# Sliding-window attention and a low-rank mixer: K and Q loaded in long rows, transposed on VectorE as bf16 pairs, scores on 32-row array tiles

## The chip, the cores and the metric

One core of a Trainium2 chip. The metric is the device time of one execution in microseconds (us), lower is better. Times come with a state (slow means over 1.5% above the fastest run of the same kernel); all timed runs used here are of the fast state, except that a run with a single execution has no state. "Span" is the profiled execution from its first to its last instruction, about 1.6 to 2.1 us shorter than its time. The "granted clock" is the share of TensorE's full clock that the profile shows as granted: 1 is full, 0.5 half. Engines: PE is TensorE's matmuls, PEld its weight loads, DVE VectorE, ACT ScalarE, POOL GpSimd.

## The reference, cut to what matters

```python
# q, k, v: (8 batches, 8 heads, 576, 64); window 64
scores = scale * q @ k^T;  mask: 0 <= i - j < 64
x = softmax(scores) @ v            # -> (8, 576, 512)
u = x + (U V applied along the sequence)
out = u + relu(u @ w_ch1) @ w_ch2  # 512 -> 2048 -> 512
```

All 4608 tokens go through the last line in nine chunks of 512. Attention of batch c+1 is woven into the matmuls of chunk c, in numbered slots; batch 0's stands alone ahead of chunk 0. I call that part the start-up; it ends with the first up-projection matmul (tile `psA`).

## The kernel before

K and Q are loaded in bf16 with the sequence on partitions, in pieces of 64 elements (groups of six rows for batches 0 and 1), transposed on TensorE against an identity, and evacuated by ScalarE (K) and VectorE (Q). A score matmul takes 128 keys, two heads on two 64-row tiles of the array. Cuts are marked `...`.

```python
def tr(src, j, wide=False):        # batches 2 to 7 take this path
    ...
    tp = ps_tp.tile([P, NT, P], BF16, name="tpn", tag="tp")
    for t in range(NT):
        nc.tensor.transpose(tp[:, t, :], src[:, t, 2*j : 2*j+2, :]..., ident[:])
def TK(j): nc.scalar.copy(out=like(kt[j][:]), in_=tr(kb, j))
def TQ(j): nc.vector.tensor_copy(out=like(qt[j][:]), in_=tr(qb, j, ...))
def scores(sc, n, j, blk):
    for g in range(2):             # two heads, rows 0-63 and 64-127
        nc.tensor.matmul(sc[:, g, n*W : (n+1)*W], kt[j][rs, w0 : w0+P],
                         qt[j][rs, blk*W : (blk+1)*W], start=True, stop=True)
PLACE = {"S": [2, 2, 6, 6, 10], "PV": [13, 13, 16, 16, 18],
         "T": [16, 17, 18, 19, 20, 21, 22, 23], ...}   # slot in the chunk
```

`turn_over(n)` issues n filler matmuls whose result nobody reads; they keep TensorE busy in the start-up. In the schedules, `T` or `KT` stands for transposing K and Q, `S` for a piece of scores with its exponential on ScalarE and its mask product on VectorE, `VC` for copies of V, `PV` for a value tile, `U` and `V` for the low-rank mixer, and `UT` for transposing the tokens.

The softmax here doesn't subtract the row's maximum and nothing guards it: scores larger than these inputs give would overflow.

Of the kernel before, what the change touches and what calls it, by code (L numbers as in the profile page):

```python
# [9 lines left out]
ALU = mybir.AluOpType  # L10
# [6 lines left out]
def kernel(  # L17
# [19 lines left out]
    HP = H // 2  # L37
# [3 lines left out]
    GR = 6  # L41
    NGR = 2
    GP = S // GR
# [14 lines left out]
    kg_pool = ctx.enter_context(tc.tile_pool(name="kg", bufs=4))  # L58
# [15 lines left out]

    ident = const.tile([P, P], BF16, name="ident")
    maskA = const.tile([P, 2, NB - 1, W], BF16, name="maskA")
    w1b = const.tile([P, NDC, F], BF16, name="w1b")
    w2b = const.tile([P, NFC, DM], BF16, name="w2b")
    NT = 5
# [7 lines left out]
    vB = [const.tile([P, NFULL, H, VW], BF16, name=f"vB{i}") for i in range(2)]  # L87
    kn = [const.tile([P, NT, H, D], BF16, name=f"kn{i}") for i in range(2)]
    qn = [const.tile([P, NT, H, D], BF16, name=f"qn{i}") for i in range(2)]
    kt = [const.tile([P, S], BF16, name=f"kt{j}") for j in range(HP)]  # L90
    qt = [const.tile([P, S], BF16, name=f"qt{j}") for j in range(HP)]
    pts = const.tile([P, HP, 2, NB, W], BF16, name="pts")

    loaded = {}


    def load_kq(b, split):
        grouped = b < NGR
        if grouped:
            kb = kg_pool.tile([GP, H, GR, D], BF16, name="kg")  # L100
            qb = kg_pool.tile([GP, H, GR, D], BF16, name="qg")
        else:
            kb, qb = kn[b % 2], qn[b % 2]
        loaded[b] = (kb, qb)
        if grouped:
            step = 2 if split else H
            for h0 in range(0, H, step):
                hs = slice(h0, h0 + step)
                for t, src in ((kb, k), (qb, q)):
                    nc.gpsimd.dma_start(  # L110
                        out=t[:, hs, :, :].rearrange("p h c d -> p h (c d)"),
                        in_=src[b, hs, :, :].rearrange("h (p c) d -> p h (c d)", c=GR),
                    )
                    yield
        else:
            for t in range(NT):
                rows = P if t < NFULL else W
                for dst, src in ((kb, k), (qb, q)):
                    nc.gpsimd.dma_start(  # L119
                        out=dst[0:rows, t, :, :],  # L120
                        in_=src[b, :, t * P : t * P + rows, :].rearrange("h p d -> p h d"),
                    )
                yield

    def load_v(b, both=False):
        va, vb = vA[b % 2], vB[b % 2]
        for t in range(NFULL):
            nc.gpsimd.dma_start(  # L128
                out=va[:, t, :, 0:D],
                in_=v[b, :, t * P : (t + 1) * P, :].rearrange("h p d -> p h d"),  # L130
            )
            if both and t > 0:
                nc.gpsimd.dma_start(  # L133
                    out=vb[:, t - 1, :, 0:D],
                    in_=v[b, :, t * P - W : t * P + W, :].rearrange("h p d -> p h d"),
                )
        lo = 0 if both else W
        nc.gpsimd.dma_start(
            out=vb[lo:P, NFULL - 1, :, 0:D],
            in_=v[b, :, NFULL * P - W + lo : S, :].rearrange("h p d -> p h d"),  # L140
        )

    def shift_v(b, copy):
        va, vb = vA[b % 2], vB[b % 2]
        for t in range(NFULL):
            if t > 0:
                copy(out=vb[W:P, t - 1, :, 0:D], in_=va[0:W, t, :, 0:D])
            copy(out=vb[0:W, t, :, 0:D], in_=va[W:P, t, :, 0:D])


    kq0 = load_kq(0, True)
    nc.vector.memset(idle[:], 0.0)  # L152
    nc.vector.memset(ident[:], 0.0)
    next(kq0)
    next(kq0)
# [450 lines left out]
```

## Time and profile before

| | before |
|---|---|
| time, median of 4 runs | 351.89 us (351.63, 351.83, 351.95; one of 492.81 is no fast run) |
| start-up (first `psA`) | 28.5 us |
| chunks 0 to 8 | 40.4, 41.0, 36.6, 36.5, 37.0, 36.5, 34.2, 27.6, 31.6 us |
| DMA packets | 132 thousand |

The chunk times are differences between the first `psA` pieces of the chunks in the chain of waits (a piece there can begin up to 0.2 us after its first matmul); the last goes to the end of the span. Lines of the profile's page, with busy us and share of the span, the granted TensorE clock in 40 slices (9 is 90% or more), and the shares of the chain of waits that ended last:

```profile
span 349.8 us, 7003 instructions
...
PE 332.9 (95%) x2963; PEld 167.0 (48%) x3014; DVE 174.5 (50%) x320; ACT 125.0 (36%) x191; POOL 119.5 (34%) x150
...
PEclk9999999999999999999999999999999999999999
...
PE psU L457 34%; PE psA L435 31%; DMA qg<-in_q_dram 6%; PE tpn L254 5%; PE xr L324 3%; DMA vA_103<-in_v_dram 2%; PE sc L278 2%; PE psv L373 2%; PE tpu L408 2%; PE pshh L353 1%; POOL kg L110 1%; ACT pts L293 1%; POOL qg L110 1%; POOL vA_103 L128 1%; POOL w2b L210 0%
```

TensorE is the limit and has its full clock from start to end. Its timeline, with start, duration, operation, shapes and count (read the distance between starts: a `psA` matmul is drawn 0.38 us long, but the next one starts 0.2155 us after it):

```profile
28.52 4.69 PE L435 MATMUL psA<-uTc,w1b 128*128 128x512 bf16 x21 [0.67 <-ACT uTc L413]
...
185.50 0.41 PE L278 MATMUL sc<-qt_115,kt_111 64*128 64x64 bf16 x16
185.75 0.40 PE L278 MATMUL sc<-qt_116,kt_112 64*128 64x64 bf16 x16
186.08 3.67 PE L435 MATMUL psA<-uTc,w1b 128*128 128x512 bf16 x15
...
208.11 0.44 PE L254 MATMUL tpn<-ident,qn_109 128*128 128x128 bf16 x5
208.39 0.38 PE L457 MATMUL psU<-w2b,c_8_2872 128*128 128x512 bf16 x1
```

The start-up ends at 28.52. 32 score matmuls hold TensorE from 185.50 to 186.08. Five transposes cost 0.28 us, and a batch from 2 on has eight such bursts.

### The profile page before, as it was taken

The page shows a single profiled execution, that of the slowest core. Times are in us where ns is not written, and L with a number is a line of the kernel's source. Part 1 is how long each engine was busy: PE and PEld are TensorE (multiplying, and loading weights), DVE is VectorE, ACT ScalarE, POOL GpSimd, SP SyncE. Part 2 cuts the span into 40 slices and gives each one's busy share as a digit, 9 for nine tenths or more (in the row PEclk, how much of TensorE's full clock was granted, in tenths as well). Part 3 has the DMA queues.
Part 4 walks back from the last instruction along what each step waited for, and adds up shares of the span by engine and source line. Part 5 has one row for each costly group of instructions (what it writes and reads, how often), then busy time and mean ns, then how long its engine had stood idle before and what let it go on. Part 6 is the DMA issues. An engine that isn't in the chain of part 4 may idle for free.

```text
span 349.8 us, 7003 instructions
## 1 busy us (share of the span) xinstructions
PE 332.9 (95%) x2963; PEld 167.0 (48%) x3014; DVE 174.5 (50%) x320; ACT 125.0 (36%) x191; POOL 119.5 (34%) x150
## 2 busy tenths in 40 slices
PE   7978989988999999999999999999999999999995
PEld 3434454444554455545554555445544454444442
DVE  3574257555653755375446545664546554214311
ACT  2632461355332632354225423353335231401300
POOL 8892269989944046605480160000000000000000
PEclk9999999999999999999999999999999999999999
DMA  8999999999999059906995292000010011011011
GB/s 112 166 207 207 198 142 188 167 171 143 149 127 167 2 37 134 187 24 45 108 163 66 15 131 66 32 2 30 32 62 0 32 43 49 0 60 62 0 52 69
DMA packets 132175, 31.89 MB, mean 91 GB/s; under 512 B 121264, under 2 KB 126384, under 8 KB 132144
## 3 DMA queue, kind: packets, MB, share of 16 engines
q0 software_dynamic: 125552, 21.57, 88.7%
q1 hardware_dynamic: 6592, 9.88, 8.2%
q8 instruction: 23, 0.38, 0.4%
q14 instruction: 8, 0.07, 0.1%
HBM read 43.57 MB, written 9.44 MB: 152 GB/s over the span
## 4 chain that ended last, share of the span: by engine, by line
PE 82%; DMA 9%; POOL 4%; issue 2%; ACT 1%; DVE 1%; POOLq 0%; ACTq 0%
PE psU L457 34%; PE psA L435 31%; DMA qg<-in_q_dram 6%; PE tpn L254 5%; PE xr L324 3%; DMA vA_103<-in_v_dram 2%; PE sc L278 2%; PE psv L373 2%; PE tpu L408 2%; PE pshh L353 1%; POOL kg L110 1%; ACT pts L293 1%; POOL qg L110 1%; POOL vA_103 L128 1%; POOL w2b L210 0%
## 5 line engine op out<-in xcount | busy, mean ns | idle before, releaser
L435 PE MATMUL psA<-uTc,w1b 128*128 128x512 bf16 x553 | 129.8, 379 | 2.1 <-ACT uTc L413 0.7
L435 PEld LDWEIGHTS <-w1b 128*128 128x128 bf16 x576 | 54.0, 98 | 62.6 <-issue 2.2
L466 DVE TENSOR_TENSOR osb<-psU,un 128x512 f32<-128x512 f32 x36 | 24.8, 690 | 60.5 <-PE psU L457 54.2
L293 ACT ACTIVATE pts<-sc 128x1024 bf16<-128x1024 f32 x32 | 31.4, 1023 | 17.9 <-PE sc L278 17.9
L294 DVE TENSOR_TENSOR pts<-pts,maskA 128x1024 bf16<-128x1024 bf16 x32 | 22.2, 695 | 17.8 <-ACT pts L293 17.6
L128 POOL DMA_DIRECT2D vA_104<-in_v_dram x16 | 14.2, 889 | 43.7 <-PE xr L324 35.7
L413 ACT COPY uTc<-tpu 128x512 bf16<-128x512 bf16 x27 | 15.8, 585 | 27.9 <-PE tpu L408 27.9
L128 POOL DMA_DIRECT2D vA_103<-in_v_dram x16 | 14.3, 907 | 17.0 <-PE xr L324 16.5
L333 DVE RECIPROCAL rcp<-xr 128x8 f32<-128x8 f32 (+1 forms) x40 | 8.2, 204 | 21.4 <-PE xr L324 21.2
L324 PEld LDWEIGHTS <-pts 128*64 128x64 bf16 x576 | 12.8, 110 | 12.2 <-issue 9.5
L119 POOL DMA_DIRECT2D kn_108<-in_k_dram x15 | 13.0, 866 | 9.0 <-PE tpn L254 8.5
L389 DVE TENSOR_TENSOR un<-psv,xs_102 128x512 bf16<-128x512 f32 (+1 forms) x18 | 11.9, 687 | 7.9 <-PE psv L373 7.9
L408 PEld LDWEIGHTS <-un 128*128 128x128 bf16 x144 | 10.6, 98 | 8.9 <-issue 1.9
L389 DVE TENSOR_TENSOR un<-psv,xs_101 128x512 bf16<-128x512 f32 (+1 forms) x18 | 11.5, 682 | 5.8 <-PE psv L373 5.8
L334 DVE TENSOR_TENSOR xs_102<-xr,rcp 128x512 bf16<-128x512 f32 (+1 forms) x20 | 13.8, 692 | 0.7
L334 DVE TENSOR_TENSOR xs_101<-xr,rcp 128x512 bf16<-128x512 f32 (+1 forms) x20 | 13.8, 690 | 0.7
L500 PE MATMUL unread<-idle 128*128 128x256 bf16 (+1 forms) x46 | 12.5, 371 | 1.6 <-DVE idle L152 1.3
L119 POOL DMA_DIRECT2D kn_107<-in_k_dram x15 | 12.9, 863 | 3.2 <-PE tpn L254 2.5
L119 POOL DMA_DIRECT2D qn_110<-in_q_dram x15 | 13.1, 874 | 1.4 <-PE tpn L254 1.4
L119 POOL DMA_DIRECT2D qn_109<-in_q_dram x15 | 13.0, 867 | 1.2 <-PE tpn L254 0.9
L373 PE MATMUL psv<-hh,vrep 128*128 128x512 bf16 x40 | 12.7, 379 | 0.7 <-DVE un L389 0.6
L133 POOL DMA_DIRECT2D vB_106<-in_v_dram x12 | 10.7, 892 | 6.2 <-DMA w2b<-in_moe_w_ch_dram 4.2
(579 smaller groups left out, 590.8 us busy)
## 6 DMA issues: line engine op xcount, KB each, us to landing
out_dram<-osb SPq DMA_DIRECT2D x36, 256.0 KB, 2.6
vA_103<-in_v_dram POOLq DMA_DIRECT2D x16, 128.0 KB, 6.0
w1b<-in_moe_w_ch_dram POOLq DMA_DIRECT2D x2, 1024.0 KB, 13.7
w2b<-in_moe_w_ch_dram POOLq DMA_DIRECT2D x2, 1024.0 KB, 15.3
vA_104<-in_v_dram POOLq DMA_DIRECT2D x16, 128.0 KB, 5.7
vB_106<-in_v_dram POOLq DMA_DIRECT2D x16, 128.0 KB, 5.9
kn_107<-in_k_dram POOLq DMA_DIRECT2D x12, 128.0 KB, 5.5
qn_109<-in_q_dram POOLq DMA_DIRECT2D x12, 128.0 KB, 5.6
```

What stands on the lines that cost most here:

```text
L119: nc.gpsimd.dma_start(out=dst[0:rows, t, :, :], in_=src[b, :, t * P : t * P + rows, :].rearrange("h p d -> p h d"),)
L128: nc.gpsimd.dma_start(out=va[:, t, :, 0:D], in_=v[b, :, t * P : (t + 1) * P, :].rearrange("h p d -> p h d"),)
L293: nc.scalar.activation(out=dst, in_=sc[:], func=ACT.Exp, scale=scale)
L294: nc.vector.tensor_tensor(out=dst, in0=dst, in1=maskA.rearrange("p g n w -> p g (n w)"), op=ALU.mult)
L324: nc.tensor.matmul(xr[r0 : r0 + W, h // 4, (h % 4) * VW : (h % 4 + 1) * VW], pts[:, h // 2, h % 2, blk, :], rhs, start=True, stop=True,)
L334: nc.vector.tensor_tensor(out=x[lo:hi, t, :, :].rearrange("p (a h) d -> p a h d", a=2), in0=xv[:, :, :, 0:D], in1=rcp[lo:hi].to_broadcast( ...
L373: nc.tensor.matmul(ps[:, n, :], vrep[:, off : off + P], hh["sb"][:], start=True, stop=not on_pe)
L389: nc.vector.tensor_tensor(out=u_tiles[g][rs, :], in0=ps[rs, n, :], in1=xt[n][rs], op=ALU.add)
L408: nc.tensor.transpose(tp[:, dc, :], u_tiles[g][:, dc * P : (dc + 1) * P], ident[:])
L435: nc.tensor.matmul(ps[:], w1b[:, dc, i * P : (i + 1) * P], uTc[:, dc, :], start=(dc == 0), stop=(dc == NDC - 1),)
L457: nc.tensor.matmul(acc[t][:], c1[i][:, t * P : (t + 1) * P], w2b[:, i, :], start=(i == 0), stop=(i == NFC - 1),)
L466: nc.vector.tensor_tensor(out=osb[:], in0=acc[t][:], in1=u_tiles[g][:], op=ALU.add)
```

## The change

The intent is to take the transposes off TensorE. K and Q now arrive as one head per 32-partition quadrant, 18 rows of 64 elements in one stretch per partition. VectorE transposes them as 4-byte words, each a pair of bf16; as the diff's indices have it, the head dimension lands as 32 partitions times 2. A score then needs two accumulating matmuls (`e` = 0, 1) with 32 contracted rows, for 64 keys at a time. The block's shifted copy of V is made by VectorE instead of a second load (for batch 0 instead of GpSimd's copies). The core of the diff, cut:

```diff
-    kb = kg_pool.tile([GP, H, GR, D]); ... per-tile loads of 64-element rows
+    kv = k[b].rearrange("(j i) (p c) d -> (i p) j (c d)", i=NQ, c=RP)
+    nc.gpsimd.dma_start(out=kr[b % 2][:, j], in_=kv[:, j])      # and q
-    TK / TQ: 40 TensorE transposes and 8 evacuations a batch
+    nc.vector.transpose(                                        # KT, 4 a batch
+        out=dst[:, j].rearrange("q (p c) e -> q p (c e)", c=RP).bitcast(U32)
+        .rearrange("q p c -> q c p"),
+        in_=src[odd][:, j, :].bitcast(U32).rearrange("q (c e) -> q c e", e=32))
-    nc.tensor.matmul(sc[:, g, ...], kt[j][rs, w0 : w0 + P], ...)
+    for e in range(2):
+        for half in range(2):
+            for g in range(2):
+                rs = slice((2 * p + g) * 32, (2 * p + g + 1) * 32)
+                nc.tensor.matmul(sc[half*W:(half+1)*W, g, ...],
+                    kt[rs, j, kb*W:(kb+1)*W, e], qt[rs, j, ..., e],
+                    start=(e == 0), stop=(e == 1))
+    pair_v: nc.vector.tensor_copy(vb <- va)                     # VC, 2 or 8 copies
-    "S": [2, 2, 6, 6, 10], ... "T": [16, ... 23]
+    "VC": [0], "S": [1, 3, 5, 7, 9, 11], ... "KT": [13, 15, 17, 18]
 start-up, in short:
+    KT[0:2]; mask set-up; for s in 0, 1: S[s]; turn_over(4)
+    KT[2:4];              for s in 2..5: S[s]; turn_over(4)
+    VC (8 copies); PV; U; V; UT
```

The whole diff holds more that goes with this: VectorE takes 7 instead of 8 of a chunk's 16 relus, batch 1 loses its variant of the stand-alone path, and the first weight is loaded in three pieces instead of two, with the loads in another order.

More of the change, by code (lines that the diff above doesn't have):

```diff
@@ L36 @@
     NB = S // W
-    HP = H // 2
     NDC = DM // P
@@ L40 @@
     VW = D + 1
-    GR = 6
-    NGR = 2
-    GP = S // GR
+    NJ = 2
+    NQ = H // NJ
+    RP = S // 32
+    NPC = 3
+    PB = NJ * NB // NPC
     NFULL = S // P
@@ L57 @@
     const = ctx.enter_context(tc.tile_pool(name="const", bufs=1))
-    kg_pool = ctx.enter_context(tc.tile_pool(name="kg", bufs=4))
     uT_pool = ctx.enter_context(tc.tile_pool(name="uT", bufs=3))
@@ L72 @@
     ctx.enter_context(tc.manual_schedule())
+    U32 = mybir.dt.uint32
+    NT = 5
     ident = const.tile([P, P], BF16, name="ident")
-    maskA = const.tile([P, 2, NB - 1, W], BF16, name="maskA")
+    mask = const.tile([P, NJ * NB, W], BF16, name="mask")
     w1b = const.tile([P, NDC, F], BF16, name="w1b")
     w2b = const.tile([P, NFC, DM], BF16, name="w2b")
-    NT = 5
     uf = [const.tile([P, NT, R], FP32, name=f"uf{i}") for i in range(2)]
@@ L86 @@
     vA = [const.tile([P, NFULL, H, VW], BF16, name=f"vA{i}") for i in range(2)]
-    vB = [const.tile([P, NFULL, H, VW], BF16, name=f"vB{i}") for i in range(2)]
-    kn = [const.tile([P, NT, H, D], BF16, name=f"kn{i}") for i in range(2)]
-    qn = [const.tile([P, NT, H, D], BF16, name=f"qn{i}") for i in range(2)]
-    kt = [const.tile([P, S], BF16, name=f"kt{j}") for j in range(HP)]
-    qt = [const.tile([P, S], BF16, name=f"qt{j}") for j in range(HP)]
-    pts = const.tile([P, HP, 2, NB, W], BF16, name="pts")
@@ L94 @@
-    loaded = {}
-    def load_kq(b, split):
-        grouped = b < NGR
-        if grouped:
-            kb = kg_pool.tile([GP, H, GR, D], BF16, name="kg")
-            qb = kg_pool.tile([GP, H, GR, D], BF16, name="qg")
-        else:
-            kb, qb = kn[b % 2], qn[b % 2]
-        loaded[b] = (kb, qb)
-        if grouped:
-            step = 2 if split else H
-            for h0 in range(0, H, step):
-                hs = slice(h0, h0 + step)
-                for t, src in ((kb, k), (qb, q)):
-                    nc.gpsimd.dma_start(
-                        out=t[:, hs, :, :].rearrange("p h c d -> p h (c d)"),
-                        in_=src[b, hs, :, :].rearrange("h (p c) d -> p h (c d)", c=GR),
-                    )
-                    yield
-        else:
-            for t in range(NT):
-                rows = P if t < NFULL else W
-                for dst, src in ((kb, k), (qb, q)):
-                    nc.gpsimd.dma_start(
-                        out=dst[0:rows, t, :, :],
-                        in_=src[b, :, t * P : t * P + rows, :].rearrange("h p d -> p h d"),
-                    )
-                yield
@@ L125, in load_v @@
-    def load_v(b, both=False):
+    vB = [const.tile([P, NT, H, VW], BF16, name=f"vB{i}") for i in range(2)]
+    kr = [const.tile([P, NJ, RP * D], BF16, name=f"kr{i}") for i in range(2)]
+    qr = [const.tile([P, NJ, RP * D], BF16, name=f"qr{i}") for i in range(2)]
+    kt = const.tile([P, NJ, S, 2], BF16, name="kt")
+    qt = const.tile([P, NJ, S, 2], BF16, name="qt")
+    pts = const.tile([P, 2, 2, NJ * NB, W], BF16, name="pts")
+    def load_kq(b, split):
+        kv = k[b].rearrange("(j i) (p c) d -> (i p) j (c d)", i=NQ, c=RP)
+        qv = q[b].rearrange("(j i) (p c) d -> (i p) j (c d)", i=NQ, c=RP)
+        for j in range(NJ) if split else (slice(0, NJ),):
+            for dst, s in ((kr[b % 2], kv), (qr[b % 2], qv)):
+                nc.gpsimd.dma_start(out=dst[:, j], in_=s[:, j])
@@ L126, in load_v @@
+    def load_v(b):
         va, vb = vA[b % 2], vB[b % 2]
@@ L131, in load_v, with pair_v @@
             )
-            if both and t > 0:
-                nc.gpsimd.dma_start(
-                    out=vb[:, t - 1, :, 0:D],
-                    in_=v[b, :, t * P - W : t * P + W, :].rearrange("h p d -> p h d"),
-                )
-        lo = 0 if both else W
         nc.gpsimd.dma_start(
-            out=vb[lo:P, NFULL - 1, :, 0:D],
-            in_=v[b, :, NFULL * P - W + lo : S, :].rearrange("h p d -> p h d"),
+            out=vb[0:W, NFULL, :, 0:D],
+            in_=v[b, :, NFULL * P : S, :].rearrange("h p d -> p h d"),
         )
-    def shift_v(b, copy):
+    def pair_v(b, ts):
         va, vb = vA[b % 2], vB[b % 2]
-        for t in range(NFULL):
-            if t > 0:
-                copy(out=vb[W:P, t - 1, :, 0:D], in_=va[0:W, t, :, 0:D])
-            copy(out=vb[0:W, t, :, 0:D], in_=va[W:P, t, :, 0:D])
-    kq0 = load_kq(0, True)
+        nc.vector.tensor_copy(out=vb[0:W, ts], in_=va[0:W, ts])
+        up = slice(ts.start + 1, ts.stop + 1)
+        nc.vector.tensor_copy(out=vb[W:P, up], in_=va[W:P, ts])
     nc.vector.memset(idle[:], 0.0)
+    load_kq(0, True)
     nc.vector.memset(ident[:], 0.0)
-    next(kq0)
-    next(kq0)
     nc.gpsimd.affine_select(
@@ L164 @@
     )
-    nc.vector.memset(maskA[:, 0, 0:2, :], 1.0)
-    for _ in kq0:
-        pass
+    nc.vector.memset(mask[:, 0:2, :], 1.0)
     for n, base, step, mult in ((0, 0, 1, -1), (1, -1, -1, 1), (1, W, 1, -1)):
         nc.gpsimd.affine_select(
-            out=maskA[:, 0, n, :],
-            in_=maskA[:, 0, n, :],
+            out=mask[:, n, :],
+            in_=mask[:, n, :],
             compare_op=ALU.is_ge,
@@ L181 @@
         nc.vector.memset(vB[i][:, :, :, D:VW], 1.0)
+        nc.vector.memset(vB[i][W:P, 0, :, 0:D], 0.0)
     load_v(0)
@@ L188 @@
     nc.vector.memset(xs[1][0:W, 0, :, :], 0.0)
-    for i in range(2):
-        nc.vector.memset(kn[i][W:P, NFULL, :, :], 0.0)
-        nc.vector.memset(qn[i][W:P, NFULL, :, :], 0.0)
     nc.sync.dma_start(
@@ L204 @@
     w1v = moe_w_ch1.rearrange("(c p) n -> p c n", p=P)
-    for lo, hi in ((0, 1024), (1024, 2048)):
+    for lo, hi in ((0, 512), (512, 1024), (1024, 2048)):
         nc.gpsimd.dma_start(out=w1b[:, :, lo:hi], in_=w1v[:, :, lo:hi])
-    shift_v(0, nc.gpsimd.tensor_copy)
+    load_kq(1, False)
     w2v = moe_w_ch2.rearrange("(i p) m -> p i m", p=P)
@@ L210 @@
         nc.gpsimd.dma_start(out=w2b[:, lo:hi, :], in_=w2v[:, lo:hi, :])
-    for _ in load_kq(1, False):
-        pass
-    load_v(1, both=True)
+    load_v(1)
     u_tiles = {}
@@ L221, in uT_of, with attention @@
         return uT_tiles[c]
-    def attention(b, spare=False, alone=False):
+    def attention(b, alone=False):
         odd = b % 2
-        kb, qb = loaded[b]
         va, vb = vA[odd], vB[odd]
@@ L230, in attention @@
         pcs = {}
-        grouped = b < NGR
-        turn = [0]
-        def tr(src, j, wide=False):
-            if grouped:
-                if spare and turn[0] % 3 != 0:
-                    tpb = psum["mm"].tile([P, 2 * CH], BF16, name="tpm", tag="mm")
-                    tp = tpb[:, 0:S].rearrange("d (c p) -> d c p", c=GR)
-                elif wide:
-                    tpw = ps_big.tile([P, 2, 2 * CH], BF16, name="tpw", tag="big")
-                    tp = tpw[:, 0, 0:S].rearrange("d (c p) -> d c p", c=GR)
-                else:
-                    tp = ps_tp.tile([P, GR, GP], BF16, name="tpg", tag="tp")
-                turn[0] += 1
-                for c in range(GR):
-                    for g in range(2):
-                        nc.tensor.transpose(
-                            tp[g * D : (g + 1) * D, c, :], src[:, 2 * j + g, c, :], ident[0:GP, 0:GP]
-                        )
-                return tp.rearrange("d c p -> d p c")
-            tp = ps_tp.tile([P, NT, P], BF16, name="tpn", tag="tp")
-            for t in range(NT):
-                nc.tensor.transpose(
-                    tp[:, t, :],
-                    src[:, t, 2 * j : 2 * j + 2, :].rearrange("p h d -> p (h d)"),
-                    ident[:],
-                )
-            return tp.rearrange("d t p -> d (t p)")[:, 0:S]
@@ L261, in like, with KT, f, VC @@
-        def like(ap):
-            return ap.rearrange("d (p c) -> d p c", c=GR) if grouped else ap
-        def TK(j):
+        def KT(src, dst, j):
+            def f():
+                nc.vector.transpose(
+                    out=dst[:, j].rearrange("q (p c) e -> q p (c e)", c=RP).bitcast(U32)
+                    .rearrange("q p c -> q c p"),
+                    in_=src[odd][:, j, :].bitcast(U32).rearrange("q (c e) -> q c e", e=32),
+                )
+            return f
+        def VC(ts):
@@ L265, in f @@
             def f():
-                nc.scalar.copy(out=like(kt[j][:]), in_=tr(kb, j))
+                pair_v(b, ts)
             return f
-        def TQ(j):
-            def f():
-                nc.vector.tensor_copy(out=like(qt[j][:]), in_=tr(qb, j, alone and not spare))
-            return f
-        def scores(sc, n, j, blk):
-            w0 = 0 if blk == 0 else W * (blk - 1)
-            for g in range(2):
-                rs = slice(g * D, g * D + D)
-                nc.tensor.matmul(
-                    sc[:, g, n * W : (n + 1) * W],
-                    kt[j][rs, w0 : w0 + P],
-                    qt[j][rs, blk * W : (blk + 1) * W],
-                    start=True,
-                    stop=True,
-                )
@@ L287, in SC, with steps @@
-        def SC(j):
+        def SC(p, n):
+            lo, hi = n * PB, (n + 1) * PB
+            def steps():
+                for j in range(NJ):
+                    for kb in range(NB):
+                        q0 = 0 if kb == 1 else kb
+                        a = max(lo, j * NB + q0)
+                        z = min(hi, j * NB + min(kb + 2, NB))
+                        if a < z:
+                            yield j, kb, a, z
             def f():
                 sc = ps_big.tile([P, 2, CH], FP32, name="sc", tag="big")
-                for blk in range(NB - 1):
-                    scores(sc, blk, j, blk)
-                dst = pts[:, j, :, 0 : NB - 1, :].rearrange("p g n w -> p g (n w)")
-                nc.scalar.activation(out=dst, in_=sc[:], func=ACT.Exp, scale=scale)
+                todo = [[s for s in steps() if s[1] % 2 == half] for half in range(2)]
+                for r in range(max(len(x) for x in todo)):
+                    for e in range(2):
+                        for half in range(2):
+                            if r >= len(todo[half]):
+                                continue
+                            j, kb, a, z = todo[half][r]
+                            for g in range(2):
+                                rs = slice((2 * p + g) * 32, (2 * p + g + 1) * 32)
+                                nc.tensor.matmul(
+                                    sc[half * W : (half + 1) * W, g, (a - lo) * W : (z - lo) * W],
+                                    kt[rs, j, kb * W : (kb + 1) * W, e],
+                                    qt[rs, j, (a - j * NB) * W : (z - j * NB) * W, e],
+                                    start=(e == 0),
+                                    stop=(e == 1),
+                                )
+                dst = pts[:, p, :, lo:hi, :]
+                nc.scalar.activation(
+                    out=dst,
+                    in_=sc[:, :, 0 : PB * W].rearrange("p g (n w) -> p g n w", w=W),
+                    func=ACT.Exp,
+                    scale=scale,
+                )
@@ L294, in f @@
                 nc.vector.tensor_tensor(
-                    out=dst, in0=dst, in1=maskA.rearrange("p g n w -> p g (n w)"), op=ALU.mult
-                )
-            return f
-        def SC8():
-            sc = ps_big.tile([P, 2, CH], FP32, name="sc8", tag="big")
-            for j in range(HP):
-                scores(sc, j, j, NB - 1)
-            dst = pts[:, :, :, NB - 1, :]
-            src = sc[:, :, 0 : HP * W].rearrange("p g (j w) -> p j g w", w=W)
-            nc.scalar.activation(out=dst, in_=src, func=ACT.Exp, scale=scale)
-            mk = maskA[:, :, 1 : 1 + HP, :].rearrange("p g j w -> p j g w")
-            nc.vector.tensor_tensor(out=dst, in0=dst, in1=mk, op=ALU.mult)
+                    out=dst,
@@ L309, in PV @@
+                    in0=dst,
+                    in1=mask[:, lo:hi, :].unsqueeze(1).to_broadcast([P, 2, PB, W]),
+                    op=ALU.mult,
+                )
+            return f
         def PV(t):
@@ L315, in f @@
                 for h in range(H):
+                    j, i = divmod(h, NQ)
                     for blk in blks:
                         r0 = ((blk + odd) % 2) * W
-                        if blk == 0:
-                            rhs = va[:, 0, h, :]
-                        elif blk % 2 == 1:
-                            rhs = va[:, blk // 2, h, :]
-                        else:
-                            rhs = vb[:, blk // 2 - 1, h, :]
+                        rhs = va[:, blk // 2, h, :] if blk % 2 else vb[:, blk // 2, h, :]
                         nc.tensor.matmul(
                             xr[r0 : r0 + W, h // 4, (h % 4) * VW : (h % 4 + 1) * VW],
-                            pts[:, h // 2, h % 2, blk, :],
+                            pts[:, i // 2, i % 2, j * NB + blk, :],
                             rhs,
@@ L401, in f @@
                 g = g0 + t
-                if alone and t % (4 if spare else 2) != 0:
+                if alone and t % 4 != 0:
                     tpb = psum["mm"].tile([P, 2 * CH], BF16, name="tpv", tag="mm")
@@ L414, in UT @@
             return f
-        pcs["T"] = [f for j in range(HP) for f in (TK(j), TQ(j))]
-        pcs["S"] = [SC(j) for j in range(HP)] + [SC8]
+        pcs["KT"] = [KT(s, d, j) for j in range(NJ) for s, d in ((kr, kt), (qr, qt))]
+        pcs["VC"] = (
+            [VC(slice(t, t + 1)) for t in range(NFULL)] if alone else [VC(slice(0, NFULL))]
+        )
+        pcs["S"] = [SC(p, n) for n in range(NPC) for p in range(2)]
         pcs["PV"] = [PV(t) for t in range(NT)]
@@ L422, in attention @@
         return pcs
-    DVE_RELU = (1, 2, 3, 5, 6, 7, 9, 11)
+    DVE_RELU = (1, 3, 5, 7, 9, 11, 13)
     def mlp(c):
@@ L475 @@
     PLACE = {
-        "S": [2, 2, 6, 6, 10],
-        "PV": [13, 13, 16, 16, 18],
-        "T": [16, 17, 18, 19, 20, 21, 22, 23],
-        "U": [20],
-        "V": [22, 23, 24],
-        "UT": [24, 25, 26, 27, 28],
+        "VC": [0],
+        "S": [1, 3, 5, 7, 9, 11],
+        "PV": [13, 14, 15, 16, 17],
+        "KT": [13, 15, 17, 18],
+        "U": [19],
+        "V": [21, 22, 23],
+        "UT": [23, 24, 25, 26, 27],
     }
     PLACE_1 = {
-        "T": [17, 17, 18, 18, 19, 19, 20, 20],
-        "S": [18, 19, 20, 21, 21],
-        "PV": [22, 23, 24, 25, 26],
-        "U": [27, 27, 27, 27, 27],
-        "V": [28, 28, 29, 29, 30],
-        "UT": [30, 30, 31, 31, 32],
+        "KT": [6, 7, 8, 9],
+        "S": [10, 12, 14, 16, 17, 18],
+        "VC": [19],
+        "PV": [21, 22, 23, 24, 25],
+        "U": [26],
+        "V": [28, 29, 30],
+        "UT": [29, 30, 31, 31, 32],
     }
     PLACE_2 = dict(PLACE)
-    PLACE_2["T"] = [0, 1, 2, 3, 4, 5, 6, 7]
-    PLACE_2["S"] = [4, 4, 8, 8, 11]
+    PLACE_2["KT"] = [0, 0, 1, 1]
+    PLACE_2["VC"] = [5]
+    PLACE_2["S"] = [2, 4, 6, 8, 10, 12]
     unread = psum["spare"].tile([P, CH], FP32, name="unread")
@@ L505 @@
     turn_over(9)
-    att = {0: attention(0, spare=True, alone=True)}
+    att = {0: attention(0, alone=True)}
     a = att[0]
-    for j in range(HP):
-        a["T"][2 * j]()
-        turn_over(2, 256)
-        if j == 1:
-            turn_over(3)
-        a["T"][2 * j + 1]()
-        turn_over(2, 256)
-        if j == 1:
-            nc.vector.tensor_copy(
-                out=maskA[:, 0, 2:, :],
-                in_=maskA[:, 0, 1:2, :].to_broadcast([P, NB - 3, W]),
-            )
-            nc.vector.tensor_copy(out=maskA[:, 1, :, :], in_=maskA[:, 0, :, :])
-        if j > 0:
-            a["S"][j - 1]()
-            turn_over(2)
-    a["S"][HP - 1]()
-    turn_over(1)
-    a["S"][HP]()
-    turn_over(3)
+    for f in a["KT"][0:2]:
+        f()
+    nc.vector.tensor_scalar(
+        out=mask[:, 2, :], in0=mask[:, 1, :], scalar1=-1.0, scalar2=1.0, op0=ALU.mult, op1=ALU.add
+    )
+    nc.vector.tensor_copy(
+        out=mask[:, 3:NB, :].rearrange("p (m n) w -> p m n w", n=2),
+        in_=mask[:, 1:3, :].unsqueeze(1).to_broadcast([P, 3, 2, W]),
+    )
+    nc.vector.tensor_copy(out=mask[:, NB : 2 * NB, :], in_=mask[:, 0:NB, :])
+    for s in range(2):
+        a["S"][s]()
+        turn_over(4)
+    for f in a["KT"][2:4]:
+        f()
+    for s in range(2, 6):
+        a["S"][s]()
+        turn_over(4)
     for i in range(2):
@@ L530 @@
     nc.scalar.copy(out=vrep[:, W : W + S], in_=vf[:])
+    for f in a["VC"]:
+        f()
     for part, n in (("PV", 2), ("U", 0), ("V", 0), ("UT", 0)):
@@ L547, in place @@
             if b not in att:
-                att[b] = attention(b, alone=(b == 1))
+                att[b] = attention(b)
             for part in parts:
@@ L555 @@
             if b == 1:
-                for _ in load_kq(2, False):
-                    pass
+                load_kq(2, False)
             if b + 1 < B:
-                load_v(b + 1, both=True)
-            if b + 2 < B and b != 2:
-                for _ in load_kq(b + 2, False):
-                    pass
+                load_v(b + 1)
+            if b + 2 < B and b > 2:
+                load_kq(b + 2, False)
+            if b == 2:
+                slots[2].append(lambda: load_kq(4, False))
+            if b == 1:
+                slots[10].append(lambda: load_kq(3, False))
             where = {1: PLACE_1, 2: PLACE_2}.get(b, PLACE)
             if b <= 2:
-                place(b, ("T",), where)
-            if b == 2:
-                slots[8].append(lambda: [None for _ in load_kq(4, False)])
-            place(b, ("S", "PV"), where)
+                place(b, ("KT",), where)
+            place(b, ("VC", "S", "PV"), where)
             if 3 <= b + 1 < B:
-                place(b + 1, ("T",), PLACE)
+                place(b + 1, ("KT",), PLACE)
             place(b, ("U", "V", "UT"), where)
```

## The prediction

> **What bounds it now.** TensorE. The page has it busy 95% of a 349.8 us span at full clock; in the chain that ended last it holds 82%. The chain's times of the first up-projection of each 512-token chunk cut the run: start-up to 28.5 us, chunk 0 40.4, chunk 1 41.0, chunks 2 to 5 36.5 to 37.0 each, chunk 6 34.2, chunks 7 and 8 (no attention) 27.6 each. So attention costs TensorE about 9 us in a steady chunk. VectorE is 50% busy, ScalarE 36%.
>
> **What the 9 us are (the timeline of 183 to 220 us).** Transposes of Q and K: 8 bursts of 5, about 0.285 us each, plus 0.3 to 0.4 us of waits: 2.6 us (in the chain 4.5% = 15.7 us for six batches). Scores: 72 matmuls in three bursts, 0.67 + 0.72 + 0.37 = 1.76 us, that is about 15.6 ns a matmul and 0.17 to 0.25 us for entering and leaving a burst. Values 1.9, the rest 2.8.
>
> **What the change does.**
> - Transposes leave TensorE (432 pairs of weight load and matmul), with their 64 evacuations (ACT 638 ns, DVE 450 ns). In their place stand four vector transposes a batch. [...]
> - Scores become 160 matmuls a batch (1280 for 576), of 32 rows by 64 columns of the array and mostly 128 moving columns, four tiles at once, in six bursts, not three. [...] at today's 16 ns a pair, 2.6 us. With six entries of 0.2 us: 3.7 us (3.3 to 5), against 1.76.
> - A steady chunk thus gains 2.6 and loses 2.0: about -0.6 us. Over six batches -4 us.
> - Chunk 0 also loses its 96 small transposes (2.3 us) and most of about 3 us of waits there, pays 1.6 us more for scores: -3 us.
> - The second V load becomes VectorE copies; packets fall by more than half. Nothing in the steady chunks waits for DMA: worth little.
> - Start-up: [...] six score pieces with four fillers each (1.5 us apart), and eight V copies (0.3 us) stand ahead of the value evacuations on VectorE. I estimate the first up-projection at 31 us (28 to 33): +2.5 us.
>
> **Sum.** -4 - 3 + 2.5, about -4.5 us: 347.5 us. Range 339 to 357. Faster by over 2%: 0.36; within: 0.49; slower: 0.15.
>
> **What would show it.** No transposes of Q and K on TensorE; score bursts of 24 to 28 matmuls in 0.55 to 0.75 us; vector transposes near 0.75 us; steady chunks at 35.5 to 36.5 us, chunk 0 near 37, chunk 1 near 36; the first up-projection near 31 us; chunks 7 and 8 unchanged at 27.6.
>
> **What would make it wrong.** If fewer than four tiles overlap[...] a score matmul costs 25 to 30 ns and a chunk loses 1.5 us: slower. If entering a 32-row burst is cheap and overlap full, scores cost 3 us and the gain reaches 9 us. If vector transposes with their scattered writes cost 1.3 us or more, the value evacuations of slots 13 to 18 back up and TensorE waits for score or value buffers.

The forecast's 0.75 us for a vector transpose is the author's estimate only. Its 3.7 us for scores was the cut 2.5 plus six entries of 0.2; with the 2.6 that is left (160 matmuls at 16 ns, an estimate from the trace's 0.25 us for 16) it would be 3.8. The 25 to 30 ns of the failure case are an estimate as well: 128 columns at the trace's 0.2155 us for 512, two tiles at a time, come to 27 ns.

## The result, and the profile after

355.30 us (353.53 to 356.59, 4 runs) against 351.89. The ratio is 1.010 with a 95% interval of 1.0067 to 1.0134; a ratio is the mean time of one kernel's fast runs over that of the other's of the same rounds, so it is not quite the ratio of the medians. The change costs 1%: the time is inside the predicted range, but on the other side of the kernel before.

The same page lines after the change:

```profile
span 354.9 us, 7506 instructions
...
PE 339.9 (96%) x3279; PEld 160.4 (45%) x3279; DVE 201.9 (57%) x339; ACT 114.4 (32%) x177; POOL 50.9 (14%) x71
...
PEclk9556999999999999999999999999999999999999
...
PE psA L377 37%; PE psU L399 36%; PE sc L230 7%; PE xr L263 4%; PE unread L445 3%; PE psv L312 3%; PE tpu L347 2%; DMA qr<-in_q_dram 2%; PE pshh L292 1%; ACT uTc L352 1%; DVE qt L195 1%; ACT pts L238 0%; DVE kt L195 0%; DVE vB L119 0%; DVE vB L117 0%
```

Two things are new: the clock is down in the second to fourth slice (8.9 to 35.5 us), and the fillers (`unread`) stand in the chain with 3%. By stretches the two traces compare so:

| | start-up | chunk 0 | 1 | 2 | 3 | 4 | 5 | 6 | 7 | 8 |
|---|---|---|---|---|---|---|---|---|---|---|
| before | 28.5 | 40.4 | 41.0 | 36.6 | 36.5 | 37.0 | 36.5 | 34.2 | 27.6 | 31.6 |
| after | 39.7 | 38.3 | 36.2 | 36.4 | 36.2 | 36.4 | 36.2 | 36.4 | 27.6 | 31.5 |

Chunks 1 to 6 gain 4.0 us in sum, the number predicted (its parts are another matter, see below), chunk 0 gains 2.1, and the start-up loses 11.2. So the whole loss lies in the first 40 us. The stretch views of the two start-ups show it in one line each (the second ends 0.7 us before the start-up does; columns: stretch, its us, busy us of PE, PEld, DVE, ACT, POOL with counts, granted clock, DMA share, GB/s). Before:

```profile
0.00:28.50 28.50, 22.64 (x314) 11.47 (x319) 16.16 (x43) 12.03 (x18) 22.81 (x37) 1.00 1.30 165
```

After:

```profile
0.00:39.00 39.00, 30.01 (x305) 13.33 (x305) 20.87 (x51) 9.51 (x14) 18.00 (x30) 0.69 1.34 179
```

TensorE's timeline after the change, in the start-up and in a steady chunk:

```profile
8.86 0.85 PE L230 MATMUL sc<-qt,kt 32*64 32x128 bf16 x24 [3.62 <-DVE qt L195]
9.64 1.89 PE L445 MATMUL unread<-idle 128*128 128x512 bf16 x4
11.46 0.85 PE L230 MATMUL sc<-qt,kt 32*64 32x128 bf16 x24
12.24 1.89 PE L445 MATMUL unread<-idle 128*128 128x512 bf16 x4
14.06 0.54 PE L230 MATMUL sc<-qt,kt 32*64 32x128 bf16 x16
16.07 0.54 PE L230 MATMUL sc<-qt,kt 32*64 32x128 bf16 x12 [1.47 <-DVE qt L195]
16.53 1.89 PE L445 MATMUL unread<-idle 128*128 128x512 bf16 x4
18.35 0.85 PE L230 MATMUL sc<-qt,kt 32*64 32x128 bf16 x28
...
39.69 4.48 PE L377 MATMUL psA<-uTc,w1b 128*128 128x512 bf16 x20 [0.67 <-ACT uTc L352]
...
188.42 0.54 PE L230 MATMUL sc<-qt,kt 32*64 32x128 bf16 x24
188.90 1.90 PE L377 MATMUL psA<-uTc,w1b 128*128 128x512 bf16 x8
190.73 0.54 PE L230 MATMUL sc<-qt,kt 32*64 32x128 bf16 x24
```

TensorE first waits 3.6 us for the transposed Q. From then on four fillers of 512 columns take about 1.8 us (9.64 to 11.46), twice the 0.86 us they cost at full clock, and each score piece 0.8 instead of 0.5. Pieces follow each other every 2.6 us, and the chain runs through them: the fillers meant to hide a wait have become the wait. In the steady chunk eight `psA` matmuls (1.73 us) and one score burst come every 2.31 us, so a burst costs 0.58 us.

VectorE's timeline in the same start-up:

```profile
6.03 1.26 DVE L195 STREAM_TRANSPOSE kt<-kr 128x576 uint32<-128x576 uint32 x1 [1.55 <-DMA kr<-in_k_dram]
7.55 1.26 DVE L195 STREAM_TRANSPOSE qt<-qr 128x576 uint32<-128x576 uint32 x1 [0.26 <-DMA qr<-in_q_dram]
...
13.21 0.56 DVE L244 TENSOR_TENSOR pts<-pts,mask 128x768 bf16<-128x768 bf16 x1 [2.05 <-ACT pts L238]
13.68 1.25 DVE L195 STREAM_TRANSPOSE kt<-kr 128x576 uint32<-128x576 uint32 x1
14.78 1.24 DVE L195 STREAM_TRANSPOSE qt<-qr 128x576 uint32<-128x576 uint32 x1
...
25.80 0.28 DVE L117 COPY vB<-vA 64x520 bf16<-64x520 bf16 x1
...
28.34 0.21 DVE L272 RECIPROCAL rcp<-xr 128x8 f32<-128x8 f32 x1
```

The last line is where the evacuation of the value tiles begins. In the kernel before it began 10 us earlier:

```profile
18.28 0.21 DVE L333 RECIPROCAL rcp<-xr 128x8 f32<-128x8 f32 x1
```

A transpose takes 1.25 us, not the 0.75 of the prediction, and the second pair stands behind two mask products in VectorE's order, although its data had landed by 10.8 us (where POOL's wait for it ends). Eight V copies then hold VectorE from 25.8 to 28.3 us.

The kernel's own executions give a first hint of what the clock is worth. Sorted by mean granted clock, its four were 0.990, 0.978, 0.975 and 0.964 and took 353.53, 355.20, 355.40 and 356.59 us. A line through the ends gives 0.118 us per thousandth; carried to a full clock, an estimate of 352.4 us. A median run's start-up loses 3.4 + 6.1 = 9.5 us (the time lost and the gain of the chunks); by this estimate the clock could explain about 3 of them, not the rest.

### The profile page after: what moved, and what is told of

It reads as the page before. It is cut to its first block, busy times and chain, and to the rows that moved or that the text cites. A ratio compares the mean times of both kernels' runs of the same rounds, so it can differ in the third digit from the quotient of the medians.

```text
span 354.9 us, 7506 instructions
## 1 busy us (share of the span) xinstructions
PE 339.9 (96%) x3279; PEld 160.4 (45%) x3279; DVE 201.9 (57%) x339; ACT 114.4 (32%) x177; POOL 50.9 (14%) x71
## 3 DMA queue, kind: packets, MB, share of 16 engines
q0 software_dynamic: 45552, 18.35, 47.4%
## 4 chain that ended last, share of the span: by engine, by line
PE 93%; DVE 2%; DMA 2%; ACT 1%; issue 1%; POOL 0%; POOLq 0%
PE psA L377 37%; PE psU L399 36%; PE sc L230 7%; PE xr L263 4%; PE unread L445 3%; PE psv L312 3%; PE tpu L347 2%; DMA qr<-in_q_dram 2%; PE pshh L292 1%; ACT uTc L352 1%; DVE qt L195 1%; ACT pts L238 0%; DVE kt L195 0%; DVE vB L119 0%; DVE vB L117 0%
## 5 line engine op out<-in xcount | busy, mean ns | idle before, releaser
L399 PE MATMUL psU<-w2b,c 128*128 128x512 bf16 x576 | 137.4, 380 | 0.0
L399 PEld LDWEIGHTS <-c 128*128 128x128 bf16 x576 | 52.4, 98 | 57.5 <-issue 3.0
L388 ACT ACTIVATE c<-psA 128x512 bf16<-128x512 f32 x81 | 48.4, 597 | 91.0 <-PE psA L377 90.8
L386 DVE TENSOR_SCALAR c<-psA 128x512 bf16<-128x512 f32 x63 | 43.5, 690 | 32.7 <-PE psA L377 32.5
L238 ACT ACTIVATE pts<-sc 128x768 bf16<-128x768 f32 x48 | 38.9, 810 | 41.7 <-PE sc L230 41.7
L244 DVE TENSOR_TENSOR pts<-pts,mask 128x768 bf16<-128x768 bf16 x48 | 26.8, 558 | 37.9 <-ACT pts L238 37.9
L106 POOL DMA_DIRECT2D vA<-in_v_dram x32 | 28.1, 880 | 123.7 <-PE xr L263 99.3
L230 PE MATMUL sc<-qt,kt 32*64 32x128 bf16 (+2 forms) x1280 | 28.3, 223 | 5.1 <-DVE qt L195 5.1
L328 DVE TENSOR_TENSOR un<-psv,xs 128x512 bf16<-128x512 f32 (+1 forms) x38 | 24.8, 685 | 7.6 <-PE psv L312 7.5
L273 DVE TENSOR_TENSOR xs<-xr,rcp 128x512 bf16<-128x512 f32 (+1 forms) x40 | 27.6, 691 | 1.5
L195 DVE STREAM_TRANSPOSE kt<-kr 128x576 uint32<-128x576 uint32 x16 | 20.0, 1248 | 1.6 <-DMA kr<-in_k_dram 1.6
L195 DVE STREAM_TRANSPOSE qt<-qr 128x576 uint32<-128x576 uint32 x16 | 19.8, 1240 | 0.3 <-DMA qr<-in_q_dram 0.3
L347 PEld LDWEIGHTS <-un 128*128 128x128 bf16 x144 | 10.8, 98 | 9.5 <-issue 2.3
```

What stands on the lines that cost most here:

```text
L106: nc.gpsimd.dma_start(out=va[:, t, :, 0:D], in_=v[b, :, t * P : (t + 1) * P, :].rearrange("h p d -> p h d"),)
L195: nc.vector.transpose(out=dst[:, j].rearrange("q (p c) e -> q p (c e)", c=RP).bitcast(U32) .rearrange("q p c -> q c p"), in_=src[odd][:, j ...
L230: nc.tensor.matmul(sc[half * W : (half + 1) * W, g, (a - lo) * W : (z - lo) * W], kt[rs, j, kb * W : (kb + 1) * W, e], qt[rs, j, (a - j * ...
L238: nc.scalar.activation(out=dst, in_=sc[:, :, 0 : PB * W].rearrange("p g (n w) -> p g n w", w=W), func=ACT.Exp, scale=scale,)
L244: nc.vector.tensor_tensor(out=dst, in0=dst, in1=mask[:, lo:hi, :].unsqueeze(1).to_broadcast([P, 2, PB, W]), op=ALU.mult,)
L273: nc.vector.tensor_tensor(out=x[lo:hi, t, :, :].rearrange("p (a h) d -> p a h d", a=2), in0=xv[:, :, :, 0:D], in1=rcp[lo:hi].to_broadcast( ...
```

## The experiments

Three reasons compete. A: the low clock. B: the chain on VectorE (slow transposes, their place behind masks, eight V copies ahead of the first value tile). C: the fillers themselves, which stand on the chain.

"Rest" is the span minus the start-up.

| run | time, us | ratio to before, interval | start-up | rest | clock of the profiled run |
|---|---|---|---|---|---|
| before | 351.3 to 352.5 (medians) | 1 | 28.5 | 321.3 | 1.00 |
| changed | 355.30 | 1.010 (1.007 to 1.013) | 39.7 | 315.2 | 0.964 |
| e10 changed, again | 355.21 | 1.008 (1.003 to 1.013) | 38.1 | 315.1 | 0.976 |
| e1 hold the clock | 351.21 | 1.000 (0.998 to 1.001) | 34.7 | 315.2 | 1.00 |
| e2 no fillers | 349.43 | 0.994 (0.993 to 0.996) | 32.4 | 315.2 | 0.975 |
| e3 reorder | 348.23 | 0.992 (0.989 to 0.995) | 33.0 | 315.1 | 0.985 |
| e4 dense writes | 350.80 (one run) | - | 34.0 | 315.1 | 0.990 |
| e8 hold, dense writes | 350.34 (one run) | - | 33.5 | 315.1 | 1.00 |
| e5 reorder, no fillers | 345.90 | 0.982 (0.979 to 0.986) | 28.7 | 315.2 | see e5 |
| e6 reorder, hold | 345.41 | 0.981 (0.977 to 0.985) | 28.8 | 315.2 | 0.999 |
| e11 pairs only | 348.42 | 0.989 (0.985 to 0.993) | 37.5 | 308.6 | 0.985, see e5 |
| e7 reorder, hold, pairs | 339.01 | 0.963 (0.960 to 0.966) | 28.3 | 308.6 | 0.998 |
| e9 pairs on the same rows | 343.87 | 0.976 (0.971 to 0.980) | 28.9 | 312.8 | 0.994 |

The rest is 315.1 to 315.2 us in every kernel whose chunks are those of the change. Start-up and chunks are independent sums.

All runs passed the comparison with the reference, also e4 and e8, which are wrong. The scaled scores have a standard deviation of 0.010 in the first head (computed from the inputs), so the softmax is nearly flat over the window, and a wrong order of keys hardly shows. The comparison therefore says little about the scores of any kernel here.

### e1: hold the clock

```diff
-    turn_over(9)
+    turn_over(24)
...
-    after S[1], S[5]: turn_over(4), turn_over(4)
+    after S[1], S[5]: turn_over(18), turn_over(9); after PV[1]: turn_over(8)
```

> The changed kernel with more filler matmuls in the places where its trace shows TensorE idle in start-up (24 instead of 9 at the start, 18 instead of 4 after the second score piece, 9 instead of 4 after the sixth, 8 after the second value tile); nothing else. Theory A (the start-up is lost because the clock falls to half for about 24 us of it): granted clock 1.00 or 0.99, first up-projection at 32 to 34 us instead of 39.7, time 347 to 350 us. Rival B (the chain of vector transposes, masks and V copies on VectorE sets the start-up whatever the clock): first up-projection stays at 37 us or later, 353 us or more.

Measured: clock 1.00, start-up 34.7 us, 351.2 us. The timeline of TensorE shows four fillers at full speed, then a stretch of them:

```profile
9.40 1.04 PE L445 MATMUL unread<-idle 128*128 128x512 bf16 x3
10.36 0.54 PE L230 MATMUL sc<-qt,kt 32*64 32x128 bf16 x24
10.84 4.06 PE L445 MATMUL unread<-idle 128*128 128x512 bf16 x18
14.83 0.55 PE L230 MATMUL sc<-qt,kt 32*64 32x128 bf16 x28
```

(The line of three stands for four; some matmul records are missing from a trace.) Pieces are back at 0.54 us. The time misses theory A's range by 1.2 us and rival B's by 1.8: A is worth about 4 us of the median, e1's extra fillers included, and something else keeps the start-up 6 us over that of the kernel before.

### e2: no fillers after the score pieces

```diff
     for s in range(2):
         a["S"][s]()
-        turn_over(4)
...
     for s in range(2, 6):
         a["S"][s]()
-        turn_over(4)
```

> The changed kernel without the four fillers after each score piece. Rival C (the fillers themselves stand on the chain, 1.8 us each at half clock): score pieces then follow each other every 0.9 to 1.3 us instead of 2.6, first up-projection near 33 us, time near 349 us, although the clock is at half for most of the start-up. Theory A in its strict form (fillers are what brings the clock back): the clock stays at half longer, into chunk 0, and the time stays within 2 us of the changed kernel's 355.

Measured: start-up 32.4 us, 349.4 us, at a low clock. TensorE's timeline of the score pieces:

```profile
9.07 1.05 PE L230 MATMUL sc<-qt,kt 32*64 32x128 bf16 x48 [3.79 <-DVE mask L455]
10.62 0.54 PE L230 MATMUL sc<-qt,kt 32*64 32x128 bf16 x16 [0.50 <-ACT pts L238]
14.16 0.90 PE L230 MATMUL sc<-qt,kt 32*64 32x128 bf16 x40 [3.00 <-DVE qt L195]
15.63 1.55 PE L230 MATMUL sc<-qt,kt 32*64 32x64 bf16 x56 [0.57 <-ACT pts L238]
```

All six pieces are out by 17.2 us instead of 24.4. Rival C holds, and the strict form of A falls: without fillers the clock was not lower for longer, and at half clock this start-up is 2.2 us shorter than e1's at full clock. The profile also shows what remains: 3.0 us of waiting for the second pair of transposes.

### e3: VectorE's order

```diff
-    KT[0:2]; masks; S[0]; S[1]; KT[2:4]; S[2] ... S[5]; VC[0:4]
+    masks; KT[0:4]; S[0]; S[1]; S[2]; VC[0]; S[3]; VC[1]; S[4]; VC[2]; S[5]; VC[3]
```

The four fillers after each piece are kept.

> The changed kernel with VectorE's start-up order alone changed: mask set-up ahead of the vector transposes, all four transposes together, each V copy behind a mask product instead of all eight after the last. Fillers as in the changed kernel. Rival B: the value evacuations start about 4 us earlier (24 instead of 28.3 us), first up-projection near 35 us or earlier, 350 to 351 us, at an unchanged low clock. Theory A alone: less than 1.5 us gained unless the clock also changes.

Measured: 348.2 us, start-up 33.0. The value evacuations begin at 22.7 us instead of 28.3:

```profile
22.72 0.21 DVE L272 RECIPROCAL rcp<-xr 128x8 f32<-128x8 f32 x1
```

Rival B holds as expected and by more, but in the profiled run the clock also came back earlier (0.985), so the run does not separate B from A by itself. e5 against e2 does: neither has fillers after the score pieces, the matmuls of both run at half clock at least to 21 us, and VectorE's order alone takes the start-up from 32.4 to 28.7 us. (e6 is 5.8 us under e1 at full clock, but its fillers differ too.)

### e4: dense writes (wrong result)

```diff
-    out=dst[:, j]...rearrange("q p c -> q c p")     # words 18 apart
+    out=dst[:, j].rearrange("q (c p) e -> q c (p e)", c=RP).bitcast(U32)
```

> Wrong result on purpose: the vector transposes write their output densely instead of at a step of 18 words. If the scattered writes make a transpose cost 1.25 us instead of the estimated 0.75, it falls to 0.75 us here[...]. Steady chunks unchanged at 36.2 to 36.4 us either way.

The groups of VectorE instructions (line, operation, shapes, count, busy us, mean ns, idle before):

```profile
L195 DVE STREAM_TRANSPOSE kt<-kr 128x576 uint32<-128x576 uint32 x16 | 12.3, 766 | 1.6 <-DMA kr<-in_k_dram 1.6
L195 DVE STREAM_TRANSPOSE qt<-qr 128x576 uint32<-128x576 uint32 x16 | 12.0, 750 | 0.8 <-DMA qr<-in_q_dram 0.8
```

The mean falls from 1248 and 1240 ns to 766 and 750. The estimate of 0.75 us was right for a dense write; the step of 18 words costs the other 0.5 us. The chunks keep their 315.1 us, so in the chunks that half microsecond is hidden.

### e8: hold the clock and write densely (wrong result)

The edits of e1 and e4 together.

> Wrong result on purpose: e1 (fillers that hold the clock) with the dense writes of e4, which is the start-up that the prediction had assumed: full clock and vector transposes of 0.75 us. If those two are what the prediction missed, the first up-projection comes at 31 to 33 us (e1: 34.65); if it stays above 34, the hand schedule was wrong in a third place.

Measured: 33.5 us, between the two answers, so the run is not decisive. It gains 1.2 us on e1. Part of what is left is e1's own 18 fillers, which here end at 14.1 us, 1.2 us after the second pair of transposes; I put the rest down to VectorE's order, which e8 keeps.

### e5 and e6: order with and without fillers

```diff
 e5: e3, and
-        turn_over(4)
 e6: e3, and
-    turn_over(9)
+    turn_over(22)
-        turn_over(4)
+        turn_over((2, 7, 2, 2, 2, 4)[s])
     VC[3] behind PV[0]
```

> The VectorE order of e3 and no fillers after the score pieces (9 at the start kept). All four kernels so far have 315.1 to 315.2 us from the first up-projection to the end, so only the start counts. If order and fillers are separate costs, the first up-projection comes at 28 to 30 us and the time is 343.5 to 346 us, although the clock is at half for most of the start. If the two took the same time away, it stays at 31.5 to 33 us, 347 us or more.

> The VectorE order of e3 with fillers only where TensorE would wait (22 at the start, 7 while the second pair of transposes runs, 2 elsewhere, 4 after the last piece), the last V copy moved behind the first value tile. If the clock still counts once the order is right, clock 0.99 to 1.00, first up-projection at 26.5 to 28.5 us, 342.5 to 344.5 us, at least 1 us under e5. If the clock no longer matters because exponentials, masks and V copies set the pace, it equals e5 within 0.7 us.

Measured: 345.9 and 345.4 us, start-ups 28.7 and 28.8. Order and fillers are separate costs, if not quite a sum: in the profiled runs e2 and e3 take 7.3 and 6.7 us off the start-up alone, and together they give back 11 of 11.2. The mean clock of e5 reads 1.00, and this is a trap: the clock records of e5's trace begin only at 23.6 us, and the mean counts what is not recorded as full. (e11's begin at 13.1 us; and one of e2's four executions reads 1.00, the others 0.97 to 0.98, in the same time.) TensorE's timelines show what was before; the same two fillers of 256 columns in e5:

```profile
20.34 0.61 PE L445 MATMUL unread<-idle 128*128 128x256 bf16 x2
```

and in e6:

```profile
20.80 0.39 PE L445 MATMUL unread<-idle 128*128 128x256 bf16 x2
```

So e5 runs at half clock at least up to 21 us. Its median is 0.5 us above that of e6, but their executions overlap, and the profiled start-ups differ by 0.2 us the other way: the second answer of e6's expectation. Once nothing needless stands on the chain, the clock of the start-up hardly matters here; what sets it then are, in e5's chain, the arrival of V (to 17.0 us) and, in e6's, the masks, V copies and value evacuations on VectorE.

### e7, e9, e11: score pieces in pairs

```diff
-    "S": [1, 3, 5, 7, 9, 11]       (and likewise for batches 1 and 2)
+    "S": [1, 1, 5, 5, 9, 9]
 e7: on e6; e11: on the changed kernel as it is
 e9: e7, and for batches 1 to 7
-    pcs["S"] = [SC(p, n) for n in range(NPC) for p in range(2)]
+    pcs["S"] = [SC(p, n) for p in range(2) for n in range(NPC)]
```

> e6 with two score pieces in one slot in the steady chunks, three bursts a chunk instead of six. A burst took 0.58 us in the changed kernel whether it had 24 or 28 matmuls. If entering and leaving costs 0.13 to 0.2 us of that, as the prediction had it, seven chunks gain 21 entries: 2.7 to 4 us from the first up-projection to the end (315.2 down to 311 to 312.5). If the burst is all matmul time, or the pair waits for its buffers, less than 1 us or a loss.

> e7 with the six score pieces of a steady batch in another order, so that two of the three pairs of a chunk are pieces on the same two row groups of the array (p 0 with p 0, p 1 with p 1) instead of one on rows 0 to 63 and one on rows 64 to 127. e7 gained 6.6 us after the first up-projection against e6: a pair took 0.80 to 0.86 us, two single bursts 1.16. If that is all saved entries and exits, nothing changes: 308.6 us from the first up-projection to the end. If the two pieces of a pair ran at the same time on eight tiles, two of three pairs lose that: a pair comes to about 0.95 us or more, 310 to 312 us to the end.

> The changed kernel with only the score pieces paired in the chunks, start-up untouched. If start and chunks are independent sums, it gains e7's 6.5 us against e10: 348 to 350 us with the same low clock in the start, 308.6 us from the first up-projection to the end. If the gain needed the earlier start (for instance through the arrival of the second weight), it is under 4 us.

> The changed kernel, unaltered, as a control on the chip of e9 and e11. 353.5 to 356.6 us as before, 315.2 us from the first up-projection to the end, and executions with a lower mean clock take longer (355.3 us at 0.975, 353.5 at 0.99).

e7 takes 339.0 us, 3.7% under the kernel before. e11 gains 6.8 us on its control e10, with the same 308.6 us of rest as e7: the gain needs no earlier start. It is larger than expected. A pair on e7's timeline (rows 0 to 63, then rows 64 to 127):

```profile
173.53 0.76 PE L230 MATMUL sc<-qt,kt 32*64 32x128 bf16 x48
174.22 3.63 PE L377 MATMUL psA<-uTc,w1b 128*128 128x512 bf16 x15
177.78 0.81 PE L230 MATMUL sc<-qt,kt 32*64 32x128 bf16 x56
```

and on e9's (the first pair on the same rows, the second on different ones):

```profile
177.63 0.90 PE L230 MATMUL sc<-qt,kt 32*64 32x128 bf16 x52
178.46 3.63 PE L379 MATMUL psA<-uTc,w1b 128*128 128x512 bf16 x16
182.02 0.76 PE L230 MATMUL sc<-qt,kt 32*64 32x64 bf16 x52
182.71 3.63 PE L379 MATMUL psA<-uTc,w1b 128*128 128x512 bf16 x16
186.27 0.90 PE L230 MATMUL sc<-qt,kt 32*64 32x128 bf16 x56
```

Between the starts of bursts lie 16 `psA` matmuls (where 15 are shown, one record is missing) at 0.2155 us each, 3.45 us; the rest of the distance is the pair. e7: 4.25 - 3.45 = 0.80 us (0.86 for its next pair, which has 56 matmuls instead of 48). e9 on the same rows: 4.39 - 3.45 = 0.94; on different rows 4.25 - 3.45 = 0.80. Two single bursts cost 1.16. So 0.22 us of the saving is there whatever the rows; I read it as one entry and exit less, which is the prediction's 0.2. Another 0.14 comes only when the two pieces lie on different rows of the array (0.80 against 0.94); I read it as overlap of the two, which no view shows by itself. e9's rest is 4.1 us longer than e7's, more than these pairs explain (0.2 us in each of chunks 2 to 6). Chunks 0 and 1 lost 1.5 us each (39.0 and 37.2 against 37.5 and 35.6). The new order asks for the second half of K and Q sooner, while VectorE is still transposing it. e9's view of waits from 28.95 to 105 us shows this (who waited for what: us in total, times, longest):

```profile
PE sc L230 <- DVE qt L195: 3.0, 2, 1.5
```

The two waits end at 40.62 and 72.64 us, one in each chunk; e7 has none of them in these chunks.

e10 repeats the changed kernel: 355.2 us. Its four executions again order by clock (0.981, 0.976, 0.974, 0.971: 354.25, 354.93, 355.48, 356.15 us).

## Why the prediction was wrong

**Right: what bounds the kernel, and the cost of the scores.** TensorE bounds the chunks. A score burst costs 0.58 us, predicted 0.55 to 0.75. One burst less saved 0.22 us, predicted 0.2 an entry; what the 0.22 us consists of, no run shows. Here 16 score matmuls of the kernel before took 0.25 us on two tiles, 15.6 ns each; for the 28 of a burst after, on four tiles, I estimate 0.58 - 0.22 = 0.36 us, 12.9 ns each, not the 25 to 30 of the failure case. Packets fell to 52 thousand. The TensorE transposes of K and Q are all gone, and chunks 7 and 8 did not move.

**Right in sum, partly by luck: chunks 1 to 6.** They gain 4.0 us, predicted 4. But chunk 1 gains 4.8, chunks 2 to 5 only 0.35 each where 0.6 was predicted, and chunk 6 loses 2.2. The schedule explains the pattern: the kernel before transposes two batches (2 and 3) in chunk 1 and none in chunk 6, so chunk 6 only pays for the dearer scores (2.0 in the prediction). With the prediction's own 2.6 and 2.0, chunk 1 should gain 3.2; it gained more, and the 2.4 us in which TensorE sat idle there are gone as well. That surplus of 1.6 us covers what the steady chunks and chunk 6 fall short by, 1.2.

**Nearly right: chunk 0.** Predicted -3 us, measured -2.1. The sum took "most of about 3 us of waits" as gone. The kernel before had TensorE idle for 2.4 us of that chunk, and after the change the view of waits still has it wait 1.3 us for ScalarE's copies of the transposed tokens at the end of it.

**Wrong: the start-up.** The step is "I estimate the first up-projection at 31 us (28 to 33): +2.5 us". It came at 39.7 (38.1 in the second profile). In a median run the start-up costs +9.5 us instead of +2.5; with the 0.9 us that chunk 0 lacks, this turns -4.5 into +3.4. Three parts of the step were mis-sized:

1. "six score pieces with four fillers each (1.5 us apart)" were 2.6 us apart, because four fillers took 1.8 us and the piece 0.8 at half clock. The prediction took the 1.00 of the kernel before for granted, although it moved work off TensorE just where TensorE has no other: the first 39 us had 0.69 granted, and with e1's 42 more fillers the run had 1.00. Holding the clock is worth about 4 us (e1). Leaving the fillers out is worth about 6 (e2). These overlap: both act on the same 15 us.
2. The 0.75 us for a vector transpose, the estimate, was 1.25. It held for a dense write (e4: 0.766); the write's step was named as a risk, but only for the chunks, where 1.25 us turned out to be hidden. In the start-up two pairs stand on the chain. Why words 18 apart (72 bytes) cost the 0.5 us, no run shows.
3. VectorE's order. The prediction saw that V copies stand ahead of the value evacuations, but not that the second pair of transposes waits behind two mask products for data that has landed. Putting it right is worth 7 us with the fillers in place (e3), some of it through the clock, and 3.7 us of start-up without them (e2 to e5).

With VectorE's order (3) and the fillers (1) mended, the start-up is 28.8 us, as before the change, and the 6.1 us that the chunks give are the gain: 345.4 us. The prediction's 347.5 was thus within 2 us of this kernel with a start-up in order, not of this kernel.

**Left open.** Why the clock stays low for so long once it has fallen: the trace's records of the changed kernel have it at half for 17.07 us, to 25.5 us, and then, after 3.4 us at full, for 6.83 us more. From 16.1 to 24 us TensorE has no gap (the starts above: 16.07, 16.53, 18.35 and on), and the clock is still at 0.50. How the 8.7 us between the predicted 31 and the 39.7 divide among the three parts, which overlap: with full clock and dense writes (e8) the start-up is still 33.5.

## What to carry to other kernels

Moving work from a full engine to an idle one paid in the steady part here (4.0 us in chunks 1 to 6) and lost it all in the stretch where nothing overlaps (11.2 us in the start-up); cost that stretch by itself, instruction by instruction in each engine's order, and measure its clock (here 0.69 against 1.00 before). Fillers belong where the engine waits anyway (e6: clock 0.999, start-up 28.8 us); the four placed after every score piece lay on the chain (1.8 us each time at half clock; without them the kernel took 5.9 us less, e2). Group small tiled matmuls into few bursts (here 6.5 us for three bursts a chunk instead of six), and put neighbours in a burst on different rows of the array (here 0.14 us a pair).
